# Sink attention and a two-layer network in one kernel: the sinks of two query blocks transposed in one operation

## The chip, the cores and the metric

The kernel runs on one core of a Trainium2 chip. The metric is device time in microseconds (us). The profile of one execution names the engines PE (TensorE, matmuls), PEld (its weight loads), DVE (VectorE), ACT (ScalarE), POOL (GpSimd) and SP (SyncE, which issues most transfers). L281 means line 281 of the kernel file.

## The reference: what is computed

Inputs are `q`, `k`, `v` of shape 4 x 8 x 768 x 64 (batch, heads, positions, width), two sizes (`n_sink` = 4, `window` = 128), and two weight matrices of 512 x 2048 and 2048 x 512 that arrive as 64-bit floats.

```python
scores = scale * q @ k.T                        # per batch and head, scale = 1/8
keep = (pos_k < n_sink) | ((rel >= 0) & (rel < window))     # rel = pos_q - pos_k
a = softmax(where(keep, scores, -1e9))
x = (a @ v), heads side by side: 3072 tokens x 512
h = x @ w_in
out = (max(h, 0) + log1p(exp(-abs(h)))) @ w_out             # 3072 x 512
```

A query sees the 128 keys before and with it, and the first few keys of its sequence, the sinks.

## The kernel before, in words

**Tiling.** Twelve chunks of 256 queries, three for each batch; a chunk has two query blocks of 128 (`CH` = 2, index `j`). For each of the 8 heads a query block meets two key blocks of 128 and the 8 first keys (`NS` = 8, of which the mask leaves `n_sink`). The two key blocks are folded into one 128-column row of weights (a query sees in each column either the older or the newer key), so a softmax row is 136 wide: 128 window columns and 8 sink columns.

**Number formats.** From the third chunk on (chunk 2), every matmul operand is split into a rounded part and a remainder (`_copy` into the format f32r, then `_sub`), and products are sums of such parts. The first two chunks (`EXACT` = 2) use full f32 for the attention.

**The steps of attention for head `h` of a chunk** (letters as in the kernel's order strings): `scores` (S), `softmax` (T: predicated copy L243, masked minimum L249, exponential L250), `normalise` (N: L256, L257, L264), `weights_t` (W: the 128 window columns are transposed on TensorE, L297, copied and subtracted, and GpSimd unfolds them into the two key blocks, L308 and L311), `values` (V) and `out` (O).

**The sinks.** The heads go in two groups of four (`G` = 4). Once a group, `sink_weights` (k) collects the normalised sink columns of four heads in `sa`, 128 queries x 2 blocks x 4 heads x 8 keys. `sink` (K, L277 to L290) transposes the 32 columns of each block in its own operation (L281), side by side into one PSUM tile of 32 rows x 256 queries. ScalarE copies it to rows 0 to 31 of the tile `sk` (L287, recorded at the helper's line L48), and VectorE writes the remainder to rows 32 to 63 (L289, helper L56); the exact chunks have no remainder. Rows 64 to 127 of `sk` stay zero. In `values`, one matmul with `sk` as its 256-column operand (L327) opens the sum of each head:

```python
sv = c.vs[self.b, h // G][:, h % G]
nc.tensor.matmul(x[:, 0], sv, self.sk[h // G], start=True, stop=False, ...)   # L327
```

and the matmuls with the window weights (L333) follow. `vs` holds the sink keys' values, placed once for each batch and group by `sinks` (L140, steps J and j) on GpSimd: row r of `vs` for head h holds value r only if that row belongs to head h, which the 0/1 mask `hmask` arranges (`_place`, L158). The values come by a transfer of `vs` from memory, repeated on each 32 rows (`load_sinks`, L134, issued on SP). For the split chunks the values are split too (L151, L152), rounded values go to columns 0 to 63 and remainders to 64 to 127 (two placements), and rows 64 to 127 of `vs` are zeroed from the zero rows of `sk` (L154, recorded at the helper's line L60).

**The network.** `up` (U, 24 matmuls, L459), `softplus` (F: Abs, Exp and Ln on ScalarE, L466 to L468), `gate` (P: L474 on VectorE, and the rounded part `gh`, mostly on GpSimd, L52), `residue` (R: the remainder `gl` on VectorE) and `down` (D and E, 6 matmuls each, L496 to L498) run one chunk behind the attention, one eighth of the hidden columns for each head step.

**What sets the order.** For TensorE and SP the program order stands (`ORDERED`). It is the string `START` for the first two chunks, and then for each head step i one of the two strings of `STEADY`:

```python
Ctx.STEADY = ("kWUqpKSFTRDVPONE", "SWTkpUKERDNFPqVO")    # the second where i % 8 == 0
```

with `J`, `j`, `G`, `L` (sinks and loads) ahead of it. k and K act at every fourth step. So TensorE meets at K the transposes of the sinks, then S and D (or E and D), and then V, the first user of `sk`. ScalarE, VectorE and GpSimd are ordered by a planner that simulates the program and takes what is ready, earlier program steps first. `sk` of the split chunks is one tile for the whole program; the PSUM tile of the transposes is shared with those of W.

Of the kernel before, what the change touches and what calls it, by code (L numbers as in the profile page):

```python
# [11 lines left out]
F32 = mybir.dt.float32  # L12
F32R = mybir.dt.float32r
# [7 lines left out]
B, H, S, D = 4, 8, 768, 64  # L21
DM, DFF = 512, 2048
P = 128
NB = S // P
NS = 8
KW = P + NS
CH = 2
CT = CH * P
# [9 lines left out]
G = 4  # L38
# [7 lines left out]
def _copy(nc, eng, out, in_):  # L46
    if eng == "A":
        nc.scalar.copy(out, in_)  # L48
    elif eng == "V":
        nc.vector.tensor_copy(out, in_)  # L50
    else:
        nc.gpsimd.tensor_scalar(out, in_, 1.0, 0.0, ALU.mult, ALU.add)  # L52


def _sub(nc, eng, out, a, b):
    (nc.vector if eng == "V" else nc.gpsimd).tensor_tensor(out, a, b, ALU.subtract)  # L56


def _zero(nc, out, finite):
    nc.gpsimd.tensor_scalar(out, finite, 0.0, 0.0, ALU.mult, ALU.add)  # L60
# [7 lines left out]
def _constants(c):  # L68
# [6 lines left out]
    nc, cp = c.nc, c.const  # L75
# [11 lines left out]
    nc.gpsimd.iota(rel, pattern=[[-1, P]], base=0, channel_multiplier=1, allow_small_or_imprecise_dtypes=True)  # L87
    nc.gpsimd.iota(key, pattern=[[1, NS]], base=0, channel_multiplier=0, allow_small_or_imprecise_dtypes=True)
    make_identity(nc, c.ident)
    c.hmask = cp.tile([64, G], F32, name="hmask")  # L90
    nc.gpsimd.memset(c.hmask[:], 1.0)
    for e in (0, 32):
        m = c.hmask[e : e + 32]
        nc.gpsimd.affine_select(m, m, [[-NS, G]], ALU.is_ge, 0.0, base=0, channel_multiplier=1)
        nc.gpsimd.affine_select(m, m, [[NS, G]], ALU.is_ge, 0.0, base=NS - 1, channel_multiplier=-1)
# [27 lines left out]
class _Attention:  # L123
# [9 lines left out]

    def load_sinks(self):  # L134
        c, nc, b = self.c, self.c.nc, self.b
        raw = c.lp.tile([64, 2, D], F32, tag="vsr", name=f"vsr{b}", bufs=1)
        nc.sync.dma_start(raw[:], c.a["vs"][b].unsqueeze(0).broadcast_to([2, 32, 2, D]))
        c.vsr[b] = raw

    def sinks(self, g):  # L140

        c, nc, b = self.c, self.c.nc, self.b
        raw = c.vsr[b]
        if self.exact:
            c.vs[b, g] = c.lp.tile([P, G, D], F32, tag=f"vsf{g}", name=f"vsf{g}", bufs=1)
            nc.gpsimd.memset(c.vs[b, g][:], 0.0)
            self._place(c.vs[b, g][:32], raw[:32, g : g + 1], 32)
            return
        if g == 0:
            c.vsh[b] = c.lp.tile([64, 2, D], F32R, tag="vsh", name=f"vsh{b}", bufs=1)  # L150
            nc.gpsimd.tensor_scalar(c.vsh[b][:], raw[:], 1.0, 0.0, ALU.mult, ALU.add)  # L151
            nc.gpsimd.tensor_tensor(raw[:], raw[:], c.vsh[b][:], ALU.subtract)  # L152
        c.vs[b, g] = c.lp.tile([P, G, P], F32R, tag=f"vs{g}", name=f"vs{b}_{g}", bufs=1)
        _zero(nc, c.vs[b, g][64:].rearrange("p (a e) d -> p a (e d)", a=2), c.sk[64:].bitcast(F32).unsqueeze(1).broadcast_to([64, 2, CT]))  # L154
        for src, o in ((c.vsh[b], 0), (raw, D)):
            self._place(c.vs[b, g][:64, :, o : o + D], src[:, g : g + 1], 64)

    def _place(self, out, src, rows):  # L158
        self.c.nc.gpsimd.tensor_tensor(
# [117 lines left out]
    def sink(self, g):  # L277
        c, nc, chunk, sa = self.c, self.c.nc, self.chunk, self.sa
        t = c.ps_t.tile([P, CT], F32, tag="t", name=f"ts{chunk}_{g}")
        for j in range(CH):  # L280
            nc.tensor.transpose(t[: G * NS, j * P : j * P + P], sa[:, j].rearrange("p g s -> p (g s)"), c.ident[:])  # L281
        if self.exact:
            sk = c.sp.tile([P, CT], F32, tag="tl", name=f"sk{chunk}_{g}", bufs=1)[:]
            nc.gpsimd.memset(sk, 0.0)
        else:
            sk = c.sk[:]
        _copy(nc, "A", sk[: G * NS], t[: G * NS])  # L287
        if not self.exact:
            _sub(nc, "V", sk[G * NS : 2 * G * NS], t[: G * NS], sk[: G * NS])  # L289
        self.sk[g] = sk  # L290

    def weights_t(self, h):
# [217 lines left out]
def _fast(c):  # L510
# [68 lines left out]
    def sinks(g):  # L579
# [26 lines left out]
        "G": (call(att, "load_v", 2), 2),  # L606
        "L": (call(att, "load"), G + 2),
        "J": (sinks(0), 2),
        "j": (sinks(1), G - 1),
        "w": (dma, 0),  # L610
        **{kind: (stage(kind), 0) for kind in "acdl"},
# [292 lines left out]
```

## Time and profile before

| | |
|---|---|
| time, median of 3 runs | 740.09 us (737.24 to 740.62) |
| span of the profiled execution | 735.7 us, 13883 instructions |
| its own time beside the span | not shown separately; the runs lie 1.5 to 4.9 us above the span |
| TensorE busy / weight loads | 699.7 us (95%) / 624.8 us (85%) |
| VectorE, ScalarE, GpSimd busy | 552.6 us (75%), 446.1 us (61%), 400.7 us (54%) |
| mean granted clock of TensorE | 0.986 |

How to read the rows: a group's row gives line, engine, operation, what is written from what, shapes and a count; a row of a tile adds shortest, median and longest duration in ns and the first and last start. A row of the timeline starts with its start and its duration in us from the span's start; brackets at its end give how long the engine had sat idle and who ended that. A row of the chain of waits has start, length and what the end of the program hung on in that stretch. A row of a stretch gives busy time and instructions of PE, PEld, DVE, ACT and POOL, the granted clock, the share of the transfers' engines and GB/s.

### The profile page before, as it was taken

To read this page: it belongs to the slowest core of one execution; us is meant where nothing else is said; L and a number is where in the kernel's file an instruction comes from. 1 tells how busy PE (TensorE), PEld (TensorE's weight loads), DVE (VectorE), ACT (ScalarE), POOL (GpSimd) and SP (SyncE) were. 2 spreads that over 40 slices of the span, in tenths; PEclk is the share of its full clock that TensorE was granted. 3 is DMA by queue.
4 is the path that set the end of the run, shared out by engine and by line. 5 is a ranking of instruction groups with operands and counts; after the bars stand their busy time and mean duration, and the time that the engine had idled before them with its cause. 6 is when DMAs were issued, how large, how long until landed. Compare 5 with 4: busy or idle time off the path is not lost.

```text
span 735.7 us, 13883 instructions
## 1 busy us (share of the span) xinstructions
PE 699.7 (95%) x4489; PEld 624.8 (85%) x4489; DVE 552.6 (75%) x1608; ACT 446.1 (61%) x1098; POOL 400.7 (54%) x773
## 2 busy tenths in 40 slices
PE   4788899989999999998999999998999999999996
PEld 3567688979899999997899999997999999999995
DVE  5899997867877877876977887886887877754331
ACT  3577865655666666665666666665766756644331
POOL 4866476565555665665655655556655565553110
PEclk9899999999999999999999999999999999999999
DMA  8877611411321321321321322322222222100001
GB/s 291 310 255 235 187 40 48 126 46 44 98 67 49 105 61 54 93 63 42 92 74 49 95 69 57 95 60 61 62 74 77 83 61 76 58 13 0 30 1 35
DMA packets 40876, 63.22 MB, mean 86 GB/s; under 512 B 4634, under 2 KB 22362, under 8 KB 40794
## 3 DMA queue, kind: packets, MB, share of 16 engines
q1 hardware_dynamic: 36042, 45.47, 21.2%
q10 hardware_dynamic: 4752, 16.77, 6.5%
q8 instruction: 38, 0.62, 0.4%
q14 instruction: 44, 0.36, 0.2%
HBM read 55.93 MB, written 6.29 MB: 85 GB/s over the span
## 4 chain that ended last, share of the span: by engine, by line
PE 83%; DVE 6%; POOL 4%; ACT 3%; DMA 1%; issue 1%; ACTq 0%; SPq 0%; POOLq 0%; DVEq 0%
PE h L459 34%; PE acc L496 11%; PE acc L498 11%; PE acc L497 11%; PE x L333 6%; PE t L297 2%; PE s L230 2%; PE s L231 2%; PE x L327 2%; PE s L227 1%; ACT a L250 1%; POOL a L264 1%; DMA wo71r<-w 1%; POOL pt L308 1%; PE ts L281 1%
## 5 line engine op out<-in xcount | busy, mean ns | idle before, releaser
L459 PE MATMUL h<-xh,wi 128*128 128x256 f32 x1536 | 254.6, 289 | 0.0
L459 PEld LDWEIGHTS h<-xh,wi 128*128 128x128 f32 x1536 | 212.3, 192 | 1.2 <-issue 0.3
L459 PE MATMUL h<-xl,wi 128*128 128x256 f32 x768 | 154.9, 284 | 0.0
L496 PE MATMUL acc<-wo,gh 128*128 128x512 f32 x384 | 153.7, 400 | 0.0
L498 PE MATMUL acc<-wo,gl 128*128 128x512 f32 x384 | 151.7, 395 | 0.7 <-DVE gl L56 0.7
L497 PE MATMUL acc<-wo,gh 128*128 128x512 f32 x384 | 151.5, 395 | 0.0
L52 POOL TENSOR_SCALAR gh<-mt 128x512 fp32r<-128x512 f32 x91 | 56.5, 621 | 166.7 <-DVE mt L474 165.4
L466 ACT ACTIVATE mt<-h 128x512 f32<-128x512 f32 x96 | 57.2, 596 | 114.2 <-PE h L459 114.2
L459 PEld LDWEIGHTS h<-xl,wi 128*128 128x128 f32 x768 | 120.0, 192 | 0.0
L264 POOL TENSOR_SCALAR a<-a,rc 128x128 f32<-128x128 f32 x180 | 71.9, 411 | 87.1 <-DVE rc L257 78.8
L250 ACT ACTIVATE a<-a,stats 128x136 f32<-128x136 f32 x192 | 75.9, 396 | 39.1 <-DVE stats L249 39.0
L474 DVE SCALAR_TENSOR_TENSOR mt<-h,mt 128x512 f32<-128x512 f32 x96 | 65.9, 687 | 42.4 <-ACT mt L468 28.2
L498 PEld LDWEIGHTS acc<-wo,gl 128*128 128x128 f32 x384 | 72.8, 189 | 17.8 <-DVE gl L56 1.2
L496 PEld LDWEIGHTS acc<-wo,gh 128*128 128x128 f32 x384 | 72.8, 190 | 12.9 <-issue 0.4
L497 PEld LDWEIGHTS acc<-wo,gh 128*128 128x128 f32 x384 | 72.9, 190 | 9.3
L56 DVE TENSOR_TENSOR gl<-mt,gh 128x512 fp32r<-128x512 f32 x96 | 70.5, 734 | 4.4 <-POOL gh L52 4.0
L467 ACT ACTIVATE mt<-mt 128x512 f32<-128x512 f32 x96 | 60.8, 633 | 3.1
L468 ACT ACTIVATE mt<-mt 128x512 f32<-128x512 f32 x96 | 60.7, 633 | 3.0
L351 DVE TENSOR_TENSOR xt<-x,xt 64x256 f32<-64x256 f32 x80 | 33.2, 415 | 38.9 <-ACT xt L48 38.9
L243 DVE COPY_PREDICATED s<-diag,s 128x128 f32<-128x128 int32 x192 | 49.1, 289 | 15.4 <-PE s L231 11.9
L48 ACT CAST qkh<-qk 128x656 fp32r<-128x656 f32 x80 | 59.3, 741 | 0.4 <-DMA qk<-qk 0.4
L333 PE MATMUL x<-pt,vv 128*128 128x256 f32 (+1 forms) x216 | 48.7, 328 | 7.9 <-POOL pt L311 7.9
(183 smaller groups left out, 1234.9 us busy)
## 6 DMA issues: line engine op xcount, KB each, us to landing
qk<-qk SPq DMA_DIRECT2D x160, 164.0 KB, 3.0
vr<-v SPq DMA_DIRECT2D x32, 192.0 KB, 2.8
out<-o SPq DMA_DIRECT2D x24, 256.0 KB, 2.3
q<-q SPq DMA_DIRECT2D x8, 256.0 KB, 4.7
vr<-v SPq DMA_DIRECT2D x16, 128.0 KB, 2.1
k<-k SPq DMA_DIRECT2D x8, 200.0 KB, 4.9
wi00r<-w ACTq DMA_DIRECT2D x1, 511.8 KB
wi01r<-w ACTq DMA_DIRECT2D x1, 511.8 KB
```

The costliest lines, as they stand in the source:

```text
L48: nc.scalar.copy(out, in_)
L56: (nc.vector if eng == "V" else nc.gpsimd).tensor_tensor(out, a, b, ALU.subtract)
L250: nc.scalar.activation(a, a, AF.Exp, bias=nm, scale=-1.0, accum_out=sm[:, j : j + 1])
L264: (nc.vector if eng == "V" else nc.gpsimd).tensor_scalar(a, a, rc[:, j : j + 1], 0.0, ALU.mult, ALU.add)
L333: nc.tensor.matmul(x[:, :, o], w, pt[:, :, m], start=False, stop=n == 2, skip_group_check=True)
L459: nc.tensor.matmul(h[:, j], wt, x, start=k == 0, stop=k >= len(prods) - 2, skip_group_check=True)
L467: nc.scalar.activation(t[:], t[:], AF.Exp, scale=-1.0)
L468: nc.scalar.activation(t[:], t[:], AF.Ln, bias=1.0)
L474: nc.vector.scalar_tensor_tensor(t[:], h[:], 0.0, t[:], ALU.max, ALU.add)
L496: nc.tensor.matmul(acc[:], gh[:, j, q], wh, start=f == 0, stop=False, skip_group_check=True)
L497: nc.tensor.matmul(acc[:], gh[:, j, q], wl, start=False, stop=False, skip_group_check=True)
L498: nc.tensor.matmul(acc[:], gl[:, j, q], wh, start=False, stop=f == 2 * FP - 1, skip_group_check=True)
```

## The change

The two transposes of a group's sinks become one: `sa` as a whole, 128 queries x 64 columns, is transposed into 64 rows x 128 queries, row 32 j + r being column r of block j. The two blocks then no longer share rows. Block j is copied to rows 32 j to 32 j + 31 of `sk`, columns 128 j to 128 j + 127, and its remainder goes to rows 64 + 32 j onward, in the same columns; so there are two copies (and two subtractions) of 128 columns where there was one of 256. The rest of each row of `sk` stays zero from the start. All 128 rows of `sk` can now hold something, so the values are loaded four times over, the mask `hmask` and both placements cover 128 rows (64 in the exact chunks), and the zeroing of rows 64 to 127 of `vs` is left out.

```diff
-    c.hmask = cp.tile([64, G], F32, name="hmask")
+    c.hmask = cp.tile([P, G], F32, name="hmask")
...
-    for e in (0, 32):
+    for e in range(0, P, 32):
...
-        raw = c.lp.tile([64, 2, D], F32, tag="vsr", name=f"vsr{b}", bufs=1)
-        nc.sync.dma_start(raw[:], c.a["vs"][b].unsqueeze(0).broadcast_to([2, 32, 2, D]))
+        raw = c.lp.tile([P, 2, D], F32, tag="vsr", name=f"vsr{b}", bufs=1)
+        nc.sync.dma_start(raw[:], c.a["vs"][b].unsqueeze(0).broadcast_to([4, 32, 2, D]))
...
-            self._place(c.vs[b, g][:32], raw[:32, g : g + 1], 32)
+            self._place(c.vs[b, g][:64], raw[:64, g : g + 1], 64)
...
-            c.vsh[b] = c.lp.tile([64, 2, D], F32R, tag="vsh", name=f"vsh{b}", bufs=1)
+            c.vsh[b] = c.lp.tile([P, 2, D], F32R, tag="vsh", name=f"vsh{b}", bufs=1)
...
-        _zero(nc, c.vs[b, g][64:].rearrange("p (a e) d -> p a (e d)", a=2), c.sk[64:].bitcast(F32).unsqueeze(1).broadcast_to([64, 2, CT]))
         for src, o in ((c.vsh[b], 0), (raw, D)):
-            self._place(c.vs[b, g][:64, :, o : o + D], src[:, g : g + 1], 64)
+            self._place(c.vs[b, g][:, :, o : o + D], src[:, g : g + 1], P)
...
-        for j in range(CH):
-            nc.tensor.transpose(t[: G * NS, j * P : j * P + P], sa[:, j].rearrange("p g s -> p (g s)"), c.ident[:])
+        nc.tensor.transpose(t[: CH * G * NS, :P], sa[:].rearrange("p j g s -> p (j g s)"), c.ident[:])
...
-        _copy(nc, "A", sk[: G * NS], t[: G * NS])
-        if not self.exact:
-            _sub(nc, "V", sk[G * NS : 2 * G * NS], t[: G * NS], sk[: G * NS])
+        for j in range(CH):
+            r, q = slice(j * G * NS, (j + 1) * G * NS), slice(j * P, j * P + P)
+            _copy(nc, "A", sk[r, q], t[r, :P])
+            if not self.exact:
+                _sub(nc, "V", sk[P // 2 + r.start : P // 2 + r.stop, q], t[r, :P], sk[r, q])
```

## The prediction

> **What bounds the kernel now.** I read the page of the profile first: the shares of the slices and of the chain that ended last.
>
> ```profile
> PE   4788899989999999998999999998999999999996
> PE 83%; DVE 6%; POOL 4%; ACT 3%; DMA 1%; issue 1%; ACTq 0%; SPq 0%; POOLq 0%; DVEq 0%
> PE x L333 <- POOL pt L311: 9.8, 6, 2.4
> ```
>
> TensorE is full in nearly every slice after the start, and the chain runs through it for 83%. So a matmul taken away is worth its own step, and work added to ScalarE, VectorE or GpSimd costs something only where TensorE waits for it. The view of waits (total us, times, longest) names the longest wait that this change can touch: in six places the value matmuls wait for GpSimd's masked weights, 9.8 us together. Next I read the tile that holds the transposed sinks.
>
> ```profile
> L281 PEld LDWEIGHTS ts<-ident,sa x48: 93/95/103, 17.3 to 655.2; 128*32 128x32 f32 x48
> L281 PE MATMUL ts<-ident,sa x48: 269/271/417, 17.4 to 655.3; 128*32 128x128 f32 x48
> L48 ACT CAST sk<-ts x20: 357/361/362, 117.0 to 655.6; 32x256 fp32r<-32x256 f32 x20
> L56 DVE TENSOR_TENSOR sk<-ts,sk x20: 412/414/415, 117.4 to 656.0; 32x256 fp32r<-32x256 f32 x20
> L48 ACT COPY sk<-ts x4: 344/348/361, 18.4 to 86.4; 32x256 f32<-32x256 f32 x4
> ```
>
> There are 24 sinks (12 chunks of two groups of heads), each with two transposes and one copy; 20 have a subtraction too, and the 4 of the exact chunks have none.
>
> **Part 1, one transpose for two.** The array is loaded with 64 columns for 32, and the same 128 columns of the identity pass. A transpose shows 271 ns but overlaps its neighbours; its step is read from the chain (start, us, what):
>
> ```profile
> 176.74 0.22 PE ts L281 x2
> 176.96 0.23 PE acc L496
> ```
>
> 0.11 us for each. The 20 sinks of the steady part lie between matmuls that do not wait, so 20 x 0.11 = 2.2 us come off. The wider load is not in the trace for this tile; it lies between 95 ns and the 132 ns of 64-column loads elsewhere, and the matmuls ahead cover it.
>
> ```profile
> L327 PEld LDWEIGHTS x<-sk,vsf x32: 132/136/227, 21.8 to 110.1; 128*64 128x64 f32 x32
> ```
>
>  If nothing covered it, 20 x 0.04 us would be lost and 1.4 us left. I take 2.2.
>
> **Part 2, two copies and two subtractions for one.** Each now spans 128 columns. Nearest rows: ScalarE's two 128-column products, VectorE's 128-column minimum.
>
> ```profile
> 23.41 0.70 ACT L262 ACTIVATE a<-a,rc 128x128 f32<-128x128 f32 x2
> 5.98 0.29 DVE L117 TENSOR_TENSOR mask<-mask,mask_room 128x128 f32<-128x128 f32 x1
> ```
>
> Two copies take 0.70 us for 0.36; two subtractions 0.58 for 0.41, and the first can run beside the second copy. The end of the second subtraction is 0.70 + 0.03 + 0.29 = 1.02 us after the copy began, against 144.85 + 0.41 - 144.45 = 0.81 before: 0.2 us later, less 0.11 for the earlier transpose. What stands behind is seen at a second group (first block) and at a first group (second block):
>
> ```profile
> 144.45 0.36 ACT L48 CAST sk<-ts 32x256 fp32r<-32x256 f32 x1 [1.66 <-PE ts L281]
> 144.85 0.41 DVE L56 TENSOR_TENSOR sk<-ts,sk 32x256 fp32r<-32x256 f32 x1 [0.94 <-ACT sk L48]
> 145.19 0.47 DVE L243 COPY_PREDICATED s<-diag,s 128x128 f32<-128x128 int32 x2
> 146.13 0.69 DVE L56 TENSOR_TENSOR gl<-mt,gh 128x512 fp32r<-128x512 f32 x1
> 146.13 0.29 PE L327 MATMUL x<-sk,vs 128*128 128x256 f32 x1
> ```
>
> ```profile
> 518.41 0.41 DVE L56 TENSOR_TENSOR sk<-ts,sk 32x256 fp32r<-32x256 f32 x1
> 518.86 0.69 DVE L56 TENSOR_TENSOR gl<-mt,gh 128x512 fp32r<-128x512 f32 x1
> 519.83 0.28 PE L327 MATMUL x<-sk,vs 128*128 128x256 f32 x1
> ```
>
> The sink matmul starts 0.87 us after the subtraction ends (145.26 to 146.13), 1.01 us in the first group. So 0.1 to 0.2 us more is covered by the down matmuls in between; without them it would be 20 x 0.1 to 0.2 us, 2 to 4 us. The second subtraction adds a wait for the second copy. Queued behind it on VectorE are the next head's predicated copy (L243) and the residue (L56 gl); behind the copies on ScalarE the Abs of the softplus (L466). They come 0.2 to 0.3 us later, and TensorE wants them an iteration or more later: nothing.
>
> In the exact chunks the matmul does wait for the copy at two of the four sinks:
>
> ```profile
> 33.09 0.65 PE L327 MATMUL x<-sk,vsf 128*64 128x256 f32 x2 [0.51 <-ACT sk L48]
> 49.08 0.65 PE L327 MATMUL x<-sk,vsf 128*64 128x256 f32 x2 [2.18 <-ACT sk L48]
> ```
>
> There the second copy's 0.34 us lies open, less 0.11 at the first: 0.57 us together; bounds 0.2 and 0.7. I take **+0.5**.
>
> **Part 3, GpSimd's zeroing goes.** Eight times, twice a batch, the zeros of the lower half (L60) are dropped, and the two placements (L159) fill 128 rows. Whether rows cost GpSimd time:
>
> ```profile
> L159 POOL TENSOR_TENSOR vs<-vsr,hmask x8: 604/605/608, 104.7 to 522.7; 64x256 fp32r<-64x256 f32 x8
> L159 POOL TENSOR_TENSOR vsf<-vsr,hmask x2: 602/602/603, 8.4 to 9.4; 32x256 f32<-32x256 f32 x2
> L56 POOL TENSOR_TENSOR xl<-xf,xh x30: 737/744/750, 128.0 to 666.0; 128x256 fp32r<-128x256 f32 x30
> ```
>
> 602 ns on 32 rows and 605 on 64: rows are free. The only 128-row, 256-wide two-operand row is 744 ns, without a repeated operand. Bounds 605 and 744; I take 605, the same instruction. The split of the sinks (L151, L152) keeps its 0.60 and 0.46 us by the same reading. Mostly this is covered by GpSimd's idle time, but at three batch changes it is on the chain:
>
> ```profile
> 158.79 0.62 POOL L60 TENSOR_SCALAR vs<-sk 64x512 fp32r<-64x512 f32 x1
> 159.46 0.69 DVE L56 TENSOR_TENSOR gl<-mt,gh 128x512 fp32r<-128x512 f32 x1
> 159.49 1.13 POOL L159 TENSOR_TENSOR vs<-vsh,hmask 64x256 fp32r<-64x256 f32 x1
> 160.58 0.60 POOL L159 TENSOR_TENSOR vs<-vsr,hmask 64x256 fp32r<-64x256 f32 x1
> 161.15 0.40 POOL L308 TENSOR_SCALAR_AFFINE_SELECT pt<-th 128x256 fp32r<-128x256 f32 x1
> 162.68 1.22 PE L333 MATMUL x<-pt,vv 128*128 128x256 f32 x3 [2.38 <-POOL pt L311]
> ```
>
> The head's masking (L308, L311) stands behind the sinks on GpSimd, and TensorE idles 2.38 us for it; the same happens at 334.23 and 504.38. Without L60 the first placement starts at 158.79, 0.70 us earlier. The second then starts 0.57 us (160.58 to 161.15) later, at 159.36, which is 0.10 us before VectorE's residue at 159.46. The first placement of before, begun 0.03 us after that residue, took 1.13 us for 0.605; begun ahead of it, neither placement is held, and the masking starts at 159.93 for 161.15: 1.22 us gained. If the residue comes first, 0.70; with placements of 744 ns and the residue first, 0.42. VectorE's residue would be late instead, by up to 0.5 us, and its product is wanted an iteration on. I take 1.2: **3 x 1.2 = 3.6 us**, bounds 1.3 and 3.7. The 0.10 us of margin is the weakest figure of the sum, since a planner sets the order on GpSimd and VectorE.
>
> On who waits here the Trainium skill (SBUF — State Buffer, section "Who interferes with whom") says that a VectorE instruction with two SBUF inputs and a GpSimd instruction that reads SBUF exclude each other, and that whichever is issued first decides. The 1.13 us row agrees; by that rule this term is 3.6 us with the placement first and 2.1 us with the residue first.
>
> **Part 4, what follows the stall.** Granted clock (the number after the busy times) in two stretches that both hold such a stall:
>
> ```profile
> 162.00:167.00 5.00, 4.32 (x17) 3.65 (x18) 2.25 (x6) 0.83 (x3) 1.95 (x6) 0.66 0.01 3
> 332.00:337.00 5.00, 2.77 (x16) 2.41 (x17) 2.06 (x6) 1.28 (x7) 3.05 (x8) 1.00 0.04 17
> ```
>
> After the first stall the clock was 0.66 for 5 us, after the second 1.00. Of the 4.32 busy us there 0.34, an estimate of 1.5 us, was lost. With a stall of 1.2 us for 2.4 this may not recur; as one of three equal stalls showed it, I take half, **0.7 us** (bounds 0 and 1.5).
> The Trainium skill (TensorE: Matmul & The Clock Gate, section "What's actually happening") says the clock falls after at least one idle window of some 3.4 us. Here 2.4 us of idling was enough, so the measurement decides; by that rule the shorter stall would change nothing, and the sum would be 0.7 us smaller.
>
> A second, smaller wait follows the second group's placements:
>
> ```profile
> 192.48 0.62 PE L333 MATMUL x<-pt,vv 128*128 128x512 f32 x2 [0.39 <-POOL pt L311]
> 183.05 2.20 DVE L56 TENSOR_TENSOR qkh<-qk,qkh 64x256 fp32r<-64x256 f32 x1
> 184.23 0.74 POOL L56 TENSOR_TENSOR vv<-vr,vv 128x256 fp32r<-128x256 f32 x1
> ```
>
> VectorE's split there ended 0.28 us after GpSimd's queue did (185.25 against 184.97). With L60 gone that queue ends some 0.5 us earlier, which covers 0.39; it happens twice (again at 362.61), **0.8 us**, bounds 0 and 0.8.
>
> **Costed at nothing.** Four more selects on the head mask (L94, L95) come once, at the start, where GpSimd is idle until the load of the sinks, and that load is 64 KB for 32, five times:
>
> ```profile
> 8.45 0.60 POOL L159 TENSOR_TENSOR vsf<-vsr,hmask 32x256 f32<-32x256 f32 x1 [3.80 <-DMA vsr<-vs]
> L94 POOL TENSOR_SCALAR_AFFINE_SELECT hmask<-hmask x2: 180/182/184, 2.4 to 2.9; 32x4 f32<-32x4 f32 x2
> GB/s 291 310 255 235 187 40 48 126 46 44 98 67 49 105 61 54 93 63 42 92 74 49 95 69 57 95 60 61 62 74 77 83 61 76 58 13 0 30 1 35
> ```
>
> 3.80 us cover 4 x 0.18; uncovered they would be 0.7 us once. The first load sits on SP's queue among the loads of keys and queries, and what is queued behind it (heads 4 to 7) comes 32 KB / 291 GB/s = 0.1 us later, at the later batches hidden by the matmuls; uncovered it would be 0.5 us in five places. The sink matmul itself has 128 rows before and after.
>
> **Sum:** -2.2 - 3.6 - 0.7 - 0.8 + 0.5 = **-6.8 us**. It is made against the profiled execution, whose span is 735.7 us; 1.5 to 4.9 us lie between it and the runs (737.24 to 740.62). I carry the difference to their median: 740.1 - 6.8 = **733.3 us**; with the bounds on either side (-8.0 to -2.0) 732.1 to 738.1.
>
> **Rivals.**
> *The gain is eaten on GpSimd.* The planner that orders GpSimd, VectorE and ScalarE puts the residue first, or 128 rows cost 744 ns: 3 x 0.42 from the stall, no clock and nothing at the second wait: -2.2 - 1.3 + 0.5 = -3.0, **737.1 us**. For it: the 0.10 us margin. Against: 602 and 605 ns.
> *The stall goes altogether.* The planner, with GpSimd shorter, lets the masking pass ahead of the sinks: 3 x 2.38 + 2 x 0.39 = 7.9 us of waiting, 1.5 us of clock and Part 1 less the exact chunks, 2.2 - 0.5: -11.1, **729 us**. For it: the masking's input was ready before the sinks were begun. Against: the sinks come earlier in the program, and nothing in the edit moves them.
> *The second subtraction lands behind the residue.* VectorE's planned order may put it after L243, the scores and the residue. In the second groups it would begin at 146.74 and end at 147.03, while the matmul now wants it at 146.02: 1.0 us open, ten times, -6.8 + 10 = +3; with the first groups some 9 us more. Between them, **747 us**. It decides from 0.87 us of lateness. For it: two halves are two chances to be overtaken. Against: its input comes 0.3 us after its twin's, before L243 has run.
> *It does not do what it says:* the 64-column transpose could take two steps; that costs 2.2 us and falls within the first rival.
>
> **How the numbers follow.** Forecast 0.50, gain eaten 0.25, stall gone 0.10, subtraction late 0.15. About 0.5% (3.7 us) is what this kernel's measurement can tell, so faster is below 736.4 and slower above 743.8. Faster: 0.45 of the forecast's 0.50, 0.05 of the eaten gain, all 0.10 of the third: 0.60. Same: 0.05 + 0.18 + 0.03 = 0.26. Slower: 0.02 + 0.12 = 0.14. The range, 728.0 to 741.5, leaves out most of the late subtraction and some of the third case; the forecast's own is 730.5 to 736.5.
>
> **What would show it.** Part 1: 24 transposes of the sinks for 48, with a step near 0.11 in the chain. Part 2: copies near 0.35 and subtractions near 0.29 us, no new wait at L327 after 110 us. Part 3: no L60 on vs, placements near 0.605, the 2.38 us stalls near 1.2. Part 4: no stretch at 0.66 behind the first batch change. Wrong it would be with a new wait of L327 for VectorE, or stalls that stay over 2 us.

## The result, and the profile after

The changed kernel takes 732.41 us (median of 5 runs, 729.96 to 734.62) against 740.09 us (737.24 to 740.62) for the kernel before on the same chip: a ratio of 0.9893, 95% interval 0.9873 to 0.9913, so 1.1% less. A second set of runs gave 0.9881 (0.9861 to 0.99). The forecast was 733.3 us, inside a range of 728.0 to 741.5, with faster as the likeliest outcome. The profiled execution of the changed kernel has a span of 728.3 us and took 729.99 us.

The page of the changed kernel: TensorE's slices, the shares of the chain that ended last, and the busy times.

```profile
span 728.3 us, 13870 instructions
PE 695.7 (96%) x4465; PEld 619.4 (85%) x4465; DVE 551.4 (76%) x1628; ACT 453.0 (62%) x1122; POOL 396.2 (54%) x769
...
PE   4888899999999999999999999999999999999996
...
PE 83%; DVE 7%; POOL 3%; ACT 3%; issue 1%; DMA 1%; ACTq 0%; SPq 0%; POOLq 0%; DVEq 0%
```

TensorE is still full and the chain still runs through it for 83%; the three slices beyond the start that showed 8 (the batch changes) now show 9. The tile of the transposed sinks (shortest, median and longest ns, first and last start) and that of the placed values have the new instructions:

```profile
L279 PEld LDWEIGHTS ts<-ident,sa x24: 110/110/128, 17.6 to 647.6; 128*64 128x64 f32 x24
L279 PE MATMUL ts<-ident,sa x24: 270/272/393, 17.6 to 647.7; 128*64 128x128 f32 x24
L48 ACT CAST sk<-ts x40: 249/256/259, 115.0 to 648.6; 32x128 fp32r<-32x128 f32 x40
L56 DVE TENSOR_TENSOR sk<-ts,sk x40: 281/284/290, 115.5 to 648.9; 32x128 fp32r<-32x128 f32 x40
```

```profile
L158 POOL TENSOR_TENSOR vs<-vsr,hmask x8: 609/612/1062, 101.8 to 515.6; 128x256 fp32r<-128x256 f32 x8
```

24 transposes for 48, of the same duration with 64 columns as with 32; copies of 256 ns and subtractions of 284 ns; placements of 612 ns on 128 rows, where 64 rows took 605.

**Where the time came from.** The matmul that opens each head's sum (L327) runs 80 times in the split chunks, once for each head step, and its starts cut that stretch into 79 steps. Its row before, and its row after:

```profile
L327 PE MATMUL x<-sk,vs x80: 279/281/288, 119.5 to 676.1; 128*128 128x256 f32 x80
```

```profile
L327 PE MATMUL x<-sk,vs x80: 278/280/389, 117.5 to 668.7; 128*128 128x256 f32 x80
```

556.6 us from the first to the 80th became 551.2 us: 5.4 of the 7.4 us by which the span shrank. The other 2.0 us lie ahead of the first (119.5 to 117.5), in the exact chunks, and nothing behind the last (59.6 us of the span in both). Step by step, from the starts of these matmuls, the differences from the kernel before are (us, summed over the steps of a kind; in brackets another execution of the changed kernel, e11, against the same execution of the kernel before; the experiments are below):

| steps | changed | Part 3 alone (e1) | Parts 1, 2 alone (e2) | copies first (e3) |
|---|---|---|---|---|
| 19 steps that hold a sink's transposes | -1.96 (-1.92) | +0.03 | -1.99 | -1.96 |
| 10 steps, from a chunk's second head to its third | +1.88 (+2.00) | -0.01 | +5.12 | -0.14 |
| 3 steps at a batch change | -3.93 (-3.88) | -4.11 | -1.46 | -4.09 |
| 2 steps with the second wait | -1.29 (-1.31) | -1.30 | -1.30 | -1.31 |
| 45 others | -0.14 (-0.17) | -0.06 | -0.14 | -0.13 |
| sum | -5.44 (-5.28) | -5.45 | +0.23 | -7.63 |

A step repeats to some 0.02 us from one execution to the next (a step with transposes: 7.15 in three executions of the kernel before, 7.04 to 7.06 in the changed one), and in the table's second row to some 0.05. Two rows depend on the execution of the kernel before. Against its other two executions, e9 and e10, the changed kernel's steady part is about 6 and 7 us shorter, for the 5.4 here: in e9 the second wait is there at three steps (7.46, 7.46 and 7.47 us) for the two here, in e10 at none, and in e10 the clock falls at all three batch changes. But for that, this table tells apart what the times of whole runs, which spread by 3 to 5 us, cannot. In the changed kernel the transposes gave what was forecast for them, and the second row took nearly all of it away.

### The profile page after: what moved, and what is told of

Its sections match the earlier page's. It is cut to its first block, busy times and chain, and to the rows that moved or that the text cites. A ratio compares the mean times of both kernels' runs of the same rounds, so it can differ in the third digit from the quotient of the medians.

```text
span 728.3 us, 13870 instructions
## 1 busy us (share of the span) xinstructions
PE 695.7 (96%) x4465; PEld 619.4 (85%) x4465; DVE 551.4 (76%) x1628; ACT 453.0 (62%) x1122; POOL 396.2 (54%) x769
## 4 chain that ended last, share of the span: by engine, by line
PE 83%; DVE 7%; POOL 3%; ACT 3%; issue 1%; DMA 1%; ACTq 0%; SPq 0%; POOLq 0%; DVEq 0%
PE h L459 33%; PE acc L496 11%; PE acc L497 11%; PE acc L498 11%; PE x L333 6%; PE s L229 2%; PE t L297 2%; PE s L230 2%; PE x L327 2%; PE s L226 2%; ACT a L249 1%; DVE wt L403 1%; DVE s L242 1%; POOL a L263 1%; POOL pt L308 1%
## 5 line engine op out<-in xcount | busy, mean ns | idle before, releaser
L466 ACT ACTIVATE mt<-h 128x512 f32<-128x512 f32 x96 | 57.5, 599 | 104.0 <-PE h L459 103.5
L474 DVE SCALAR_TENSOR_TENSOR mt<-h,mt 128x512 f32<-128x512 f32 x96 | 65.8, 685 | 47.2 <-ACT mt L468 34.6
L249 ACT ACTIVATE a<-a,stats 128x136 f32<-128x136 f32 x192 | 76.0, 397 | 38.5 <-DVE stats L248 38.5
L498 PEld LDWEIGHTS acc<-wo,gl 128*128 128x128 f32 x384 | 72.2, 188 | 17.8 <-DVE gl L56 1.3
L56 DVE TENSOR_TENSOR gl<-mt,gh 128x512 fp32r<-128x512 f32 x96 | 72.9, 759 | 4.9 <-POOL gh L52 4.6
L56 DVE TENSOR_TENSOR kl<-qk,qkh 128x400 fp32r<-128x400 f32 x80 | 52.3, 654 | 2.5
```

The source lines that it names most:

```text
L249: nc.scalar.activation(a, a, AF.Exp, bias=nm, scale=-1.0, accum_out=sm[:, j : j + 1])
L474: nc.vector.scalar_tensor_tensor(t[:], h[:], 0.0, t[:], ALU.max, ALU.add)
L498: nc.tensor.matmul(acc[:], gl[:, j, q], wh, start=False, stop=f == 2 * FP - 1, skip_group_check=True)
```

## The experiments

**One part each.** The first kernel has Part 3 alone (values, mask and placements on 128 rows, no zeroing; `sink` as before). The second has the whole change, but zeroes the rows again ahead of the placements.

```diff
 e1: the changed kernel, with
-        nc.tensor.transpose(t[: CH * G * NS, :P], sa[:].rearrange("p j g s -> p (j g s)"), c.ident[:])
+        for j in range(CH):
+            nc.tensor.transpose(t[: G * NS, j * P : j * P + P], sa[:, j]..., c.ident[:])
...
+        _copy(nc, "A", sk[: G * NS], t[: G * NS])
+        if not self.exact:
+            _sub(nc, "V", sk[G * NS : 2 * G * NS], t[: G * NS], sk[: G * NS])
 e2: the changed kernel, with
+        _zero(nc, c.vs[b, g][64:], c.ident[64:].unsqueeze(1).broadcast_to([64, G, P]))
```

> The kernel before with Part 3 alone: values of the sinks loaded and placed on 128 rows, no zeroing of the lower rows; sinks transposed, copied and subtracted as before. Theory (the gain is GpSimd's queue at the batch changes): the stalls of 2.38 us in front of L333 fall to some 1.6, the stretch of low clock behind the first one is gone, the 0.39 us waits too; about 0.85 x 3 + 1.4 + 0.9 = 4.9 us less, span near 731. Rival (the gain is TensorE's saved transposes and the start): 2 us or less here, span 734 or more.

> The changed kernel with one GpSimd operation of the old zeroing's size (64 rows x 512, read from the identity matrix) put back ahead of the placements, which then overwrite it: Parts 1 and 2 alone. Theory: the stalls at the batch changes are back at 2.3 us, L333 waits in the first groups' next head as in the changed kernel, span about 728.3 + 4.9 = 733, unless the clock stays high (then 731.7). Rival: 729 or less. If the 1.9 us that the changed kernel gained before its first split sink came from Part 1 and 2, they are here; if from Part 3, they are in the run with Part 3 alone.

Measured: e1 734.24 us, ratio 0.9919 (0.9897 to 0.9941); e2 739.96 us, ratio 1.0002 (0.9984 to 1.002). So Part 3 alone gives the whole gain of the steady part, and the transposes with their copies and subtractions give nothing by themselves; the -1.46 of e2's third row is the clock, which did not fall in e2, and without it they cost 1.7 us. The value matmuls behind a batch change wait 1.50 us in e1 and 2.39 us in e2 (the rows of the timeline, with the idle time in brackets):

```profile
164.09 0.74 PE L332 MATMUL x<-pt,vv 128*128 128x256 f32 x3 [1.50 <-POOL pt L310]
```

```profile
162.52 0.73 PE L334 MATMUL x<-pt,vv 128*128 128x256 f32 x3 [2.39 <-POOL pt L312]
...
184.35 0.62 PE L334 MATMUL x<-pt,vv 128*128 128x512 f32 x2 [0.81 <-POOL pt L312]
```

In e2 the second wait of before (0.39 at 192.48) is gone too, and one of 0.81 has come up one head earlier, in the step of the table's second row; that one was not expected, and with it e2's span was 735.3 us, where 731.7 was expected if the clock stays high.

**Copies first.** In the changed kernel ScalarE and VectorE take turns at a sink: copy, subtraction, copy, subtraction. e3 writes both copies ahead of both subtractions. e7 keeps the turns, but its subtraction reads the identity in place of the PSUM tile that ScalarE copies from, so it leaves the sinks' remainders out.

```diff
 e3: the changed kernel, with
-        for j in range(CH):
-            r, q = ...
+        blocks = [...]
+        for r, q in blocks:
             _copy(nc, "A", sk[r, q], t[r, :P])
-            if not self.exact:
+        if not self.exact:
+            for r, q in blocks:
                 _sub(nc, "V", sk[P // 2 + r.start : P // 2 + r.stop, q], t[r, :P], sk[r, q])
 e7: the changed kernel, with
-                _sub(nc, "V", sk[P // 2 + r.start : P // 2 + r.stop, q], t[r, :P], sk[r, q])
+                _sub(nc, "V", sk[P // 2 + r.start : P // 2 + r.stop, q], c.ident[r, :P], sk[r, q])
```

> The changed kernel with both copies of a group put ahead of both subtractions. In the changed kernel the second copy waits for the first subtraction (0.35 us) and the second subtraction for the second copy (0.32 us), so VectorE loses 0.3 us a sink, and L333 waits some 0.25 us one head later in about six of the first groups. Theory (the wait comes from the order in which the two blocks were written): no such waits, VectorE's two subtractions back to back, the six new waits gone, about 1.5 us less, span near 727. Rival (the two engines cannot use the tile side by side in any order): the first subtraction waits for the second copy instead, VectorE still has its gap or ends as late, span within 0.5 us of 728.3.

> The changed kernel in its own order, but the subtraction takes its first operand from the identity matrix in SBUF in place of the PSUM tile of the transposes; so the remainders of the sinks are left out (wrong numbers stand in their place), and the work is the same in size. Theory (the second copy waits since the kernel lets only one engine at a time read a PSUM tile): the second copy follows the first at once, about 0.26 us after it, without waiting for VectorE. Rival (the wait is for the tile sk, which both write): the second copy still starts 0.03 us after the first subtraction's end. In time within 2 us of copies first.

Measured: e3 730.15 us, ratio 0.9875 (0.9851 to 0.9899); e7 730.53 us in one run. The interval of e3 overlaps that of the changed kernel, so the runs alone don't tell them apart; the steps do: +1.88 in the second row became -0.14, and e7 has -0.09 there. (The profiled span of e3, 728.4 us, is the one that its rival named, but its first steady matmul came at 119.8 us for 117.5, by the scatter of the start that is told below.) A sink of a second group in the changed kernel, then in e3, then in e7 (timeline, ScalarE and VectorE):

```profile
142.41 0.25 ACT L48 CAST sk<-ts 32x128 fp32r<-32x128 f32 x1 [1.56 <-PE ts L279]
142.70 0.28 DVE L56 TENSOR_TENSOR sk<-ts,sk 32x128 fp32r<-32x128 f32 x1 [0.73 <-ACT sk L48]
143.01 0.26 ACT L48 CAST sk<-ts 32x128 fp32r<-32x128 f32 x1 [0.35 <-DVE sk L56]
143.30 0.29 DVE L56 TENSOR_TENSOR sk<-ts,sk 32x128 fp32r<-32x128 f32 x1 [0.32 <-ACT sk L48]
```

```profile
144.62 0.52 ACT L48 CAST sk<-ts 32x128 fp32r<-32x128 f32 x2 [1.56 <-PE ts L279]
145.17 0.58 DVE L56 TENSOR_TENSOR sk<-ts,sk 32x128 fp32r<-32x128 f32 x2 [0.99 <-ACT sk L48]
```

```profile
144.65 0.54 ACT L48 CAST sk<-ts 32x128 fp32r<-32x128 f32 x2 [1.56 <-PE ts L279]
144.94 0.81 DVE L56 TENSOR_TENSOR sk<-ident,sk 32x128 fp32r<-32x128 f32 x2 [0.73 <-ACT sk L48]
```

With the turns, the second copy does not follow the first: it waits 0.35 us, until the first subtraction is done, and the second subtraction waits 0.32 us for it. From the first copy's start to the last subtraction's end that is 1.18 us, and VectorE stands still for 0.32 us in the middle. When the subtraction does not read the PSUM tile (e7), the second copy follows at once. So the wait is for the tile that both engines read, though each block has rows of its own in it. The timeline names the first subtraction as what released the copy, and it reads that from semaphores: as far as it tells, the wait stands in the program, put in by the kernel's dependency tracking. It orders e3's engines as well (there the first subtraction starts behind the second copy, at 0.55 us in place of 0.29), but as VectorE then runs its two subtractions back to back, nothing stands still between them. What the chip would do without that wait wasn't tried. The Trainium skill (PSUM — Partial Sum Buffer, section "PSUM bank collisions raise a hardware error") says that two engines on one bank collide only within one quadrant of 32 partitions, reads against reads included; by that the two blocks could be read at the same time. No run here shows it.

At this second group e3 ends hardly sooner than the changed kernel (1.13 us behind the first copy's start, for 1.18), and nothing is paid here. The turns are paid at the first groups. There VectorE comes to the sink late, and until its first subtraction is done the second copy holds all of ScalarE's queue. One such group in the changed kernel and the head after it, then in e3, then in the kernel before (timeline):

```profile
229.23 0.26 ACT L48 CAST sk<-ts 32x128 fp32r<-32x128 f32 x1 [1.26 <-DVE sk L56]
229.51 0.60 ACT L466 ACTIVATE mt<-h 128x512 f32<-128x512 f32 x1
230.11 0.28 PE L327 MATMUL x<-sk,vs 128*128 128x256 f32 x1
231.47 0.69 DVE L474 SCALAR_TENSOR_TENSOR mt<-h,mt 128x512 f32<-128x512 f32 x1 [0.66 <-ACT mt L468]
...
234.05 0.41 DVE L56 TENSOR_TENSOR tl<-t,th 128x256 f32<-128x256 f32 x1
...
235.92 0.42 PEld L333 LDWEIGHTS x<-pt,vv 128*128 128x128 f32 x3 [0.31 <-POOL pt L311]
```

```profile
230.16 0.60 ACT L467 ACTIVATE mt<-h 128x512 f32<-128x512 f32 x1
232.00 0.28 PE L328 MATMUL x<-sk,vs 128*128 128x256 f32 x1
232.42 0.69 DVE L475 SCALAR_TENSOR_TENSOR mt<-h,mt 128x512 f32<-128x512 f32 x1
```

```profile
232.95 0.58 ACT L466 ACTIVATE mt<-h 128x512 f32<-128x512 f32 x1
235.17 0.28 PE L327 MATMUL x<-sk,vs 128*128 128x256 f32 x1
```

The sink matmul itself (230.11) has 0.30 us to spare. But behind the second copy on ScalarE stands the softplus: its Abs (L466) begins 0.60 us ahead of the sink matmul, where it began 2.22 us ahead of it in the kernel before and 1.84 in e3. So VectorE's gate (L474) stands 0.66 us for the softplus, and what follows it is late: the remainder `tl` of the next head's weights begins 3.94 us behind the sink matmul, for 3.17 in e3 and in the kernel before. GpSimd's masking needs `tl`, and TensorE's weight load waits 0.31 us for the masking. ScalarE's stand of 1.25 to 1.26 us and the gate's of 0.66 are there at nine of the changed kernel's ten first groups, and at none of e3's (at the first of the ten the gate waits longer, in all three kernels); VectorE does its work in the same order in all three kernels. The longer work of two subtractions, 0.58 us for 0.41, is not what reaches TensorE: e3 has it as well.

The weight loads' waits between 115 and 660 us (total us, times, longest) in the changed kernel, and in e3:

```profile
PEld x L333 <- POOL pt L311: 7.8, 11, 1.9
```

```profile
PEld x L334 <- POOL pt L312: 5.5, 3, 1.8
```

Eleven waits against three, 2.3 us more. They are the three batch changes, which both kernels have, and eight more of 0.18 to 0.37 us, all at a chunk's second head, in the steps of the table's second row. These steps are 0.07 to 0.34 us longer than before in nine of the ten chunks and unchanged in the last.

**When the sinks' values are placed.** `J` and `j` stand ahead of a head step's other work. e4 puts both behind it, e5 (with e3's order of copies) only `J`, the first group's, which is the one with the split.

```diff
 e4: the changed kernel, with
-            for part in "JjGL" + c.STEADY[i % H == 0]:
+            for part in "GL" + c.STEADY[i % H == 0] + "Jj":
 e5: e3, with
+            for part in "jGL" + c.STEADY[i % H == 0] + "J":
```

> The changed kernel with the two steps that place the sinks moved from the front of a head step to its end, from the third chunk on, so that GpSimd masks the head's weights first. Theory (the rest of the stall at a batch change is the head's masking queued behind the split and placements of the sinks, 2.3 us on GpSimd): the three waits of 1.56 us at L333 go or fall under 0.3, 3 to 4.5 us less, span 724 to 725.5. Rival (GpSimd is late there for other reasons, the remainder and the normalisation ahead of it): the wait stays over 1 us, span within 1.5 us of 728.3.

> Copies first (as in that run) and, of the two steps that place the sinks, only the first group's moved to the end of the head step; the second group's stays in front. In the run with both moved, the batch change was 0.9 us shorter, but the second group's placements made new waits of 0.7 to 0.9 us at L333 two heads on (1.1 us on three intervals and on the one from the fifth to the sixth sink). Theory: those new waits come from the second group's step alone, so they are gone here, the three batch changes stay 0.8 us shorter: 2.4 us less than with copies first alone, about 535.6 - 7.8 - 2.4 = 528 us from the fifth to the last sink's transpose, 527 to 728 us median in time. Rival: the head's masking at a batch change then waits for something else, and the interval is within 0.5 us of copies first.

> Copies first and the first group's sinks at the end of the head step, a second time: the steady part again near 528.6 us from the fifth to the last sink's transpose, the time again near 727; the start 97 or 99.8 by the race (theory), 99.8 again if the program fixes it (rival).

Measured: e4 733.02 us, ratio 0.9914 (0.9893 to 0.9935); e5 726.88 us, ratio 0.9817 (0.9795 to 0.9839), and again 727.35 us, ratio 0.9826 (0.98 to 0.9852). e5 is faster than both kernels. e4 falls short of what was expected of it, waits under 0.3 us at the batch changes and a span of 724 to 725.5 us: its span is 729.8. Both move the batch change's stall one head later and shorten it, but e4 gains a new wait at the second groups (timeline of e4, then of e5):

```profile
167.36 0.74 PE L333 MATMUL x<-pt,vv 128*128 128x256 f32 x3 [0.69 <-POOL pt L311]
...
184.50 0.74 POOL L56 TENSOR_TENSOR xl<-xf,xh 128x256 fp32r<-128x256 f32 x1 [0.54 <-ACT xh L48]
...
189.36 0.62 PE L333 MATMUL x<-pt,vv 128*128 128x512 f32 x2 [0.93 <-POOL pt L311]
```

```profile
165.94 0.30 POOL L151 TENSOR_SCALAR vsh<-vsr 128x128 fp32r<-128x128 f32 x1
...
168.40 0.40 POOL L309 TENSOR_SCALAR_AFFINE_SELECT pt<-th 128x256 fp32r<-128x256 f32 x1
...
170.39 0.73 PE L334 MATMUL x<-pt,vv 128*128 128x256 f32 x3 [0.71 <-POOL pt L312]
```

In e5 the step with the old stall takes 6.94 us (before 9.60, changed 8.77) and the one behind it 9.42 (8.53, 8.42), in sum 0.83 us less than in the changed kernel at each batch change, and 9.86 us less than before over the 79 steps. The masking (168.40) did not pass ahead of the sinks (165.94) in e5 either. What differs is the head step that the sinks fall into: in the old one GpSimd has the remainder `xl` (0.74 us) as well, in the new one it hasn't. In e4 the second group's placements were moved into a step with `xl` (184.50), and there a wait arises. That `xl` is what decides is read from the two timelines; no run moved `xl` alone.

**The exact chunks, and the scatter of the start.** The 2.0 us ahead of the first steady matmul were not forecast. e6 leaves the exact chunks' sinks as before; the others are further executions of the two kernels.

```diff
 e6: the changed kernel, with, in sink(),
         if self.exact:
+            for j in range(CH):
+                nc.tensor.transpose(t[: G * NS, j * P : j * P + P], sa[:, j]..., c.ident[:])
...
+            _copy(nc, "A", sk[: G * NS], t[: G * NS])
...
 and, in sinks(),
-            self._place(c.vs[b, g][:64], raw[:64, g : g + 1], 64)
+            self._place(c.vs[b, g][:32], raw[:32, g : g + 1], 32)
```

> The changed kernel with the sinks of the two exact chunks as before (two transposes, one copy of 256 columns, placements on 32 rows). The changed kernel and every run with the new sinks there took 96.3 to 97.5 us from the first to the fifth sink's transpose, the kernel before and the run with Part 3 alone 99.2 and 99.3. Theory (those 2 us come from the exact chunks' sinks, through when VectorE and GpSimd meet): 99.2 here, steady part as in the changed kernel, median about 2 us above it, 734. Rival (it is chance of the execution): 97.5 or less.

> The changed kernel once more, on the same chip as the runs sent with it, to compare them directly: 730 to 734.6, median near 732.4; about 2 us above copies first if the six small waits in the first groups' next heads are what separates them.

> The kernel before, one more execution with its profile. From the first to the fifth sink's transpose the three executions with the old sinks in the exact chunks (before, Part 3 alone, split only) took 99.1 to 99.3 us, five of the seven with the new ones 96.3 to 97.5 and two 99.4 and 99.8. Theory (a race of VectorE's weight step at 34 us with GpSimd's, which the new sinks' timing tilts but does not decide): either value can come; 99 is the likelier. Rival (the old sinks always cost the 2 us): 99.1 to 99.3 again.

> The kernel before, another execution, for the same question: theory, either 97 or 99 from the first to the fifth sink's transpose; rival, 99.1 to 99.3. The first batch change shows besides how often the clock falls behind the 2.38 us stalls: one of three stalls in the first profile.

> The changed kernel, a third execution with its profile: theory, 97 from the first to the fifth sink's transpose is the likelier, 99.4 possible; steady part 533.0 to 533.2 whatever the start. Rival (the new sinks always save the 2 us, and the two late executions differ for another reason): 96.3 to 97.5.

Measured: e6 732.45 us, ratio 0.9916 (0.9894 to 0.9937); the changed kernel again 730.79 us, ratio 0.9881 (0.9861 to 0.99), and 732.33 us; the kernel before 738.52 and 741.28 us. The first sinks' transposes start at 17.2 to 17.8 us or at 19.5 to 19.6, in both kernels now the one and now the other: 2 us of scatter that both kernels have, and a part of the spread of the runs. From there to the fifth sink, the first of the split chunks, it took 98.9 to 99.5 us in all five executions with the old sinks in the exact chunks (the kernel before three times, e1, e6), and 96.3 to 97.4 us in seven of the nine with the new ones; the other two, e5 once and e7, took 99.8 and 99.4. So in the exact chunks some 2 us go with the edit, though not in every execution; that the old sinks could have the shorter time too, as the theory for e9 and e10 had it, was not seen.

Half of it can be followed. From the second sink to the third all five old ones took 14.30 to 14.31 us, and seven new ones 13.27 to 13.29. VectorE's step on the network's weights (L403) and GpSimd's subtraction (L56) start there within 0.1 us of each other; first in the kernel before, then in the changed one (timeline):

```profile
33.64 1.27 POOL L56 TENSOR_TENSOR wo<-wt,wo 128x512 fp32r<-128x512 f32 x1
33.75 1.70 DVE L403 SCALAR_TENSOR_TENSOR wt<-wi20r,upper 128x512 int32<-128x512 int32 x1
```

```profile
33.98 0.67 DVE L403 SCALAR_TENSOR_TENSOR wt<-wi20r,upper 128x512 int32<-128x512 int32 x1
34.04 1.74 POOL L56 TENSOR_TENSOR wo<-wt,wo 128x512 fp32r<-128x512 f32 x1 [0.20 <-ACT wo L48]
```

Whoever is first runs, and the other is held. VectorE was held (1.69 to 1.71 us) in all five old ones, and in none of the nine new ones (0.67). Behind L403 VectorE has the masked minimum (L249, which is L248 in the changed kernel), and TensorE's next scores wait for it, in the kernel before and in the changed one:

```profile
36.12 1.16 PE L227 MATMUL s<-k,q 128*128 128x264 f32 x4 [1.36 <-DVE stats L249]
```

```profile
35.32 1.16 PE L226 MATMUL s<-k,q 128*128 128x264 f32 x4 [0.26 <-DVE stats L248]
```

These 1.1 us lie between the two sinks in all five old ones and not in the seven. e5 and e7 took 14.38 us there all the same, with the granted clock at 0.88. The other half lies from the third sink to the fourth, in these stretches of the kernel before, of the changed one, and of the kernel before in e10 (the granted clock is the number behind the five busy times):

```profile
46.50:84.75 38.25, 32.66 (x185) 26.73 (x184) 36.44 (x82) 29.64 (x64) 21.95 (x23) 0.91 0.78 252
```

```profile
45.70:82.90 37.20, 31.22 (x185) 25.23 (x184) 36.16 (x81) 29.55 (x65) 22.05 (x23) 0.95 0.77 258
```

```profile
49.05:86.10 37.05, 31.03 (x186) 25.84 (x185) 35.68 (x81) 29.29 (x64) 22.71 (x23) 0.95 0.83 259
```

With the clock at 0.95 the kernel before is as quick there as the changed one, so this 1 us is the clock's. The old sinks had it in four of five executions, the new ones in two of nine (38.1 and 38.4 us, again e5 and e7); why the clock falls less often with the new sinks stays open. e6 fits: its steady part is that of the changed kernel (-5.47), its exact chunks those of before (99.1), but between runs the 2 us don't stand out: its median is 1.7 us above that of the changed kernel sent with it (730.79), and the two intervals overlap.

## Why the prediction was right or wrong

The total was right, 732.4 for 733.3 us, but by terms that were off in opposite directions.

**Part 1, the transposes: right.** 0.103 us off each step that holds one (1.96 / 19), for 0.11. The wider load takes 110 ns in the tile's row, and the steps show no cost of it. The rival by which the 64-column transpose takes two steps fell with the 272 ns.

**Part 2, "nothing" in the split chunks: wrong, +1.9 us.** The step that failed is "the first can run beside the second copy". The first subtraction and the second copy never overlapped. The copies were shorter than forecast (0.26 for 0.35 us), yet the second subtraction ended 1.18 us after the first copy began at the second groups, for a forecast 1.02, and 2.08 us at nine of the ten first groups, where it had been 1.56 to 1.60. With it failed "They come 0.2 to 0.3 us later": at the first groups ScalarE stood 1.26 us with its queue, and the Abs came 1.6 us nearer to the sink matmul. TensorE wanted what hangs on it not "an iteration or more later" with room to spare, but as masked weights one head on, where the room was less than the delay. What was watched did hold: for VectorE's `sk` the load of L327 waited 0.3 us, once, in the whole steady part. e3 turns the term into the forecast's nothing, so "nothing" holds once the turns are gone. The rival of a second subtraction behind the residue fell: the waits of 1.0 us at L327 on which it rested did not come.

**Part 3, the zeroing: right in kind, too high by a third.** Forecast 1.2 us at each batch change, measured 0.83 (9.60 to 8.77). The placements took the expected 0.61 us, and came ahead of the residue, as was the doubtful point. The changed kernel at the batch change (timeline):

```profile
156.66 0.61 POOL L158 TENSOR_TENSOR vs<-vsh,hmask 128x256 fp32r<-128x256 f32 x1
157.23 0.61 POOL L158 TENSOR_TENSOR vs<-vsr,hmask 128x256 fp32r<-128x256 f32 x1
157.40 0.99 DVE L56 TENSOR_TENSOR gl<-mt,gh 128x512 fp32r<-128x512 f32 x1
157.80 0.86 POOL L308 TENSOR_SCALAR_AFFINE_SELECT pt<-th 128x256 fp32r<-128x256 f32 x1
157.95 0.28 PE L327 MATMUL x<-sk,vs 128*128 128x256 f32 x1
...
159.79 0.73 PE L333 MATMUL x<-pt,vv 128*128 128x256 f32 x3 [1.56 <-POOL pt L311]
```

The masking (L308) starts 0.15 us ahead of the sink matmul, where before it came 1.14 us behind it (161.15 and 160.01): 1.29 us gained. Then the residue, itself held (0.99 for 0.69), holds the first masking step: 0.86 for 0.40, and 0.46 us is given back. The forecast had GpSimd's next instructions at their old durations; it had followed the contention through the placements and stopped there. The Trainium skill's rule (SBUF — State Buffer, section "Who interferes with whom") agrees with these rows and with the 1.70 and 0.67 us of L403; what was missed is that the loser of one turn won the next here. e1 confirms the size without the other parts (-4.11 at the three changes, the clock's 1.4 in it).

**Part 4, the clock: right in kind, too small.** Forecast 0.7 us, half of what one loss costs; the first batch change before took 11.03 us for the 9.60 of the others, so 1.4 us came off in the profiled pair. Behind the first batch change the changed kernel's stretch shows the clock at 1.00, where before it was 0.66:

```profile
159.00:164.00 5.00, 4.21 (x28) 3.85 (x29) 2.94 (x8) 1.69 (x4) 3.06 (x9) 1.00 0.01 3
```

In three executions of the kernel before it fell after 1, 1 and 3 of the three stalls, at 1.4 to 1.6 us each: some 2.5 us an execution, an estimate from these three (7.5 us / 3). The step that failed is "I take half" of one loss, from one execution. **The second wait** went as forecast in the profiled pair, with 1.3 us for 0.8: the steps of 7.46 became 6.82, 0.64 each. That it was there twice to be won was luck of that execution: e9 has three such steps, e10 none, and the changed kernel none in its three executions. The forecast took the matmul's wait, 0.39; the weight load ahead of it had waited longer, in the kernel before:

```profile
192.48 0.30 PEld L333 LDWEIGHTS x<-pt,vv 128*128 128x128 f32 x2 [0.70 <-POOL pt L311]
```

So the load's wait, 0.70, was the nearer price. e2 shows that it also goes when the zeroing is kept, at the price of the wait one head earlier.

**The exact chunks: wrong, -2 for +0.5.** The wait that the forecast priced came out at half its size: the matmul L327 of the exact chunks waits 0.71 and 2.25 us for `sk`, 3.0 together for the 2.7 of the two rows quoted from before, so 0.3 us more for the 0.57 forecast; the two copies took 0.51 us together, not twice 0.34. (The timeline puts the 2.25 us down to GpSimd's clearing of `sk`, but that had ended 0.86 us before the matmul, and the second copy 0.09 before it.) What was left out is that two engines that start 0.1 us apart can change places: at L403 that was worth 1.0 us, more than the term, and the clock brought another in most executions. Nothing in the profile of before told which way such a turn would fall.

**The sum.** Forecast -6.8. Measured in the profiled pair: transposes -2.0 (for -2.2), Part 2 +1.9 (0), batch changes with the clock -3.9 (-4.3), second wait -1.3 (-0.8), the rest -0.1, ahead of the steady part -2.0 (+0.5): -7.4. What Part 2 took back, the exact chunks brought, and that is luck. "1.5 to 4.9 us lie between it and the runs" was too loose: in every run of the two kernels the time is 1.7 to 1.8 us above the span (729.99 and 728.3; 738.52 and 736.8; 741.28 and 739.6). The profiled execution of before was by that one of some 737.4 us, 2.7 below the median: the span's difference of 7.4 and the medians' of 7.7 agree, but partly by chance.

## What to carry to other kernels

When one long instruction is cut into two that alternate between two engines on the same PSUM tile, the halves can run in turns, as here, and where the second engine comes late, the first stands still with its whole queue. Write all of the first engine's halves ahead of the second's, and look for what stands in the queue behind the second half. When GpSimd's queue gets shorter, charge the instruction that then meets VectorE, not only the one that was held before. And cut a kernel into its repeating steps at one matmul's starts: differences of 0.1 us show there, which runs that spread by 4 us can't show.

## What the runs showed of the hardware

**The clock falls after a stall of 2.4 us, but not each time.** Of the twelve stalls of 2.38 to 2.39 us in the kernel before (three executions) and e2, five were followed by a low clock, each costing 1.4 to 1.6 us (steps of 11.03 to 11.16 us for 9.60); of the 21 stalls of 1.50 to 1.58 us in the changed kernel (three executions), e1, e3, e6 and e7, none. A stretch of the kernel before in e10, which lost it at all three batch changes:

```profile
335.00:341.00 6.00, 5.40 (x25) 4.67 (x26) 2.78 (x8) 1.69 (x4) 2.88 (x8) 0.72 0.00 0
```

So a stall shortened by 0.8 us gains more than 0.8, and the gain differs from one execution to the next. The Trainium skill (TensorE: Matmul & The Clock Gate, section "What's actually happening") has an idle window of some 3.4 us; the stalls here were shorter, and the measurement decides.

**GpSimd's time hardly depends on rows**, over all that were used: 602 ns on 32, 605 on 64, 612 on 128, for 256 elements a row.

**A held instruction can pass the delay on.** At the batch change it went from placement to residue (0.99 us for 0.69) to masking (0.86 for 0.40), without a wait for data between them; the place where a delay shows need not be the place where it began.
